# Decode block: part of the last gate's weights loaded early on ScalarE's queue, and ScalarE's eight groups written as a loop

## The chip, the cores and the metric

The kernel runs on one core of a Trainium2 chip. The metric is the time of one execution on the device, in microseconds (us). The engines are named as the profile names them: PE multiplies matrices (PEld is its loading of weights), DVE is the vector engine, ACT the scalar engine, POOL and SP the two others. SP issues nearly all transfers here. Every transfer is cut into rows, and the rows are spread over 16 DMA engines, which work side by side.

## The reference

One decode step (one new token for each of 4 sequences) through attention with a cache and a gated feed-forward layer, both modulated by a condition `c`:

```python
x = A_x                                                   # 4 x 1 x 512
mod = (_silu(c) @ w_mod).reshape(c.shape[0], 6, 1, -1)    # 512 x 3072 weights
sa, ca, ga, sb, cb, gb = (mod[:, i] for i in range(6))
h = _layernorm(x) * (1 + ca) + sa
x = x + ga * attention(h)      # 32 heads of 128 in 8 groups, last 2048 of the cached keys
h = _layernorm(x) * (1 + cb) + sb
x = x + gb * ((_silu(h @ w1) * (h @ w3)) @ w2)            # 1792 hidden columns
```

All numbers are float32. What makes it long is the reading: keys and values of 8 groups (8 x 8 MB), the projections, and the weights of the two layers, each read once.

## The kernel before, in words

**Stages.** `t0_in` (the condition `c` and the weights of the first two gates) comes first, on SP's queue; the query weights `t1_in` and the input `x` come on ACT's queue. Then SP loads keys and values of one group after the other into two buffers, `KV[0]` and `KV[1]`, 8 MB each and so of 128 rows of 64 KB, and the projections of two groups at a time into `WP`. After the last group come, in this order and all on SP's queue: `wm_in` (three gates), `f1_in`, `f2_in` in two parts (the feed-forward layer's first weights), `gb_in` (the last gate, `gb`: 128 rows of 2048 numbers), and `w2_in` in six parts (semaphores `dw0` to `dw5`). The answer leaves with one small transfer.

**What holds a load back.** SP waits before a load until its buffer is free. Before the change it counts `q_done` (PE has projected the queries, so the query weights in `WP` may go) and `o_done` (PE has finished with the values, so a `KV` buffer may go).

**One group.** PE multiplies queries and keys (`scores`, into the accumulator `bS`), DVE finds the maxima and passes their negatives on as `NB`, ACT takes the exponent (`p_sb`), PE transposes (`bP`), DVE copies to `pT`, PE multiplies with the values (`values`, into `bO`), ACT divides by the sums (`o_sb`, with `LB` of DVE), PE transposes (`bX`, counted by `x_done`), and PE projects out (`proj_out`). ACT also scales the queries (`q_sb`) that PE has projected into `bQ`; PE transposes them (`bT`, counted by `qt_done`). PE runs the groups in a loop over four pairs (the blocks `query` and `pair`, with `take`, which waits for a semaphore and takes its count away again). DVE and ACT have all eight groups written out, and the last branch leads every engine to the block `post`.

**The end.** In `post` PE multiplies the condition with the last gate's weights into `bM` (four products of 512 columns, one for each 128 of the condition's 512 numbers, each to its own four rows), ACT copies that to `gb_sb`, and PE sums the four parts into `bT`, which ACT copies to `gbJ`. The products with `w2_in` follow part by part as they land; the last part releases the last products into `bX`, then DVE's two last operations (`yt`, `y`) and the transfer of the answer.

Of the kernel before, what the change touches and what calls it, by code (L numbers as in the profile page):

```python
# [14 lines left out]
EPS = 1e-5  # L15
CHUNKS = [(j, c) for c in range(4) for j in range(4) if c < 2 or j < 3]
HEAD = 8
W2_CUTS = [0, 4, 8, 10, 12, 13, 14]
PAIRS = G // 2

# [20 lines left out]
        return (self.sem, self.n)  # L41


def block_kernel(nc, x_in, t0_in, t1_in, kv_in, w_in, wm_in, f1_in, f2_in, gb_in, w2_in, out):
    T, v, s, gp, S = nc.tensor, nc.vector, nc.scalar, nc.gpsimd, nc.sync

    def sems(names):
        return [nc.alloc_semaphore(n) for n in names.split()]

    def sb(name, cols, rows=P):  # L50
        return nc.alloc_sbuf_tensor(name, (rows, cols), F32).ap()
# [5 lines left out]
    A = Queue(nc, s, "act")  # L57
    V = Queue(nc, v, "dve")
    L = Queue(nc, gp, "pool")
    dx, dt0, dt1, dkv, dk, dva, dvb, dwo, dm, df1, df2a, df2b, dgb = sems("dx dt0 dt1 dkv dk dva dvb dwo dm df1 df2a df2b dgb")  # L60
    dw = sems(" ".join(f"dw{i}" for i in range(len(W2_CUTS) - 1)))
    z_ok, q_ok, p_ok, k_ok, va_ok, vb_ok, pt_ok, o_ok, ot_ok = sems("z_ok q_ok p_ok k_ok va_ok vb_ok pt_ok o_ok ot_ok")
    s_done, q_done, qt_done, pp_done, o_done, x_done, a_done, pe, last = sems("s_done q_done qt_done pp_done o_done x_done a_done pe last")
    (dout,) = sems("dout")

    KV = [sb("KV0", 16384), sb("KV1", 16384)]
    WP = sb("WP", 8192)
    T0 = KV[1][:, : 16 + 4096]
    x_sb = sb("x_sb", 512, B)
    ident, same, eps = sb("ident", P), sb("same", B), sb("eps", 1)  # L70
    sc, e1, e2 = sb("sc", 16), sb("e1", 16), sb("e2", 16)
    hT, h2T = sb("hT", 16), sb("h2T", 16)
    Z = sb("Z", B * 28)
    q_sb, p_sb, o_sb, a_sb, y_sb, g_sb, u_sb, gb_sb = [sb(n, 512) for n in "q_sb p_sb o_sb a_sb y_sb g_sb u_sb gb_sb".split()]
# [10 lines left out]
    bS, bQ, bT, bP, bO, bX, bA, bM = [bank(n) for n in "bS bQ bT bP bO bX bA bM".split()]  # L85


    def load(dst, src, sem):
        S.dma_start(dst, src).then_inc(sem, 16)  # L89

    load(T0, t0_in, dt0)
    s.dma_start(WP[:, 4096:], t1_in).then_inc(dt1, 16)
    s.dma_start(x_sb, x_in).then_inc(dx, 16)
    load(KV[0], kv_in[0], dkv)
    S.wait_ge(pe, 1)
    load(KV[1], kv_in[1], dk)
    for p in range(PAIRS):
        if p == PAIRS - 1:
            break
        S.wait_ge(q_done, 2 * p + 2)  # L100
        if p:
            S.wait_ge(a_done, 2 * p)
        if p < PAIRS - 2:
            load(WP, w_in[p], dwo)
        else:
            load(WP, w_in[p], dwo)
        S.wait_ge(o_done, 2 * p + 1)
        load(KV[0], kv_in[2 * p + 2], dkv)
        S.wait_ge(o_done, 2 * p + 2)
        if p < PAIRS - 2:  # L110
            load(KV[1], kv_in[2 * p + 3], dk)
    S.wait_ge(a_done, G - 2)
# [1 line left out]
    load(KV[1][:, :8192], kv_in[G - 1][:, :8192], dk)  # L114
    load(KV[1][:, 8192:14336], kv_in[G - 1][:, 8192:14336], dva)
    load(KV[1][:, 14336:], kv_in[G - 1][:, 14336:], dvb)
    S.wait_ge(o_done, G - 1)
    load(KV[0][:, :6144], wm_in, dm)
    load(KV[0][:, 6144:14336], f1_in, df1)
    S.wait_ge(o_done, G)  # L120
    load(KV[1][:, :3072], f2_in[:, :3072], df2a)
    load(KV[1][:, 3072:6144], f2_in[:, 3072:], df2b)
    load(KV[1][:, 6144:8192], gb_in, dgb)
    for a, b, sem in zip(W2_CUTS[:-1], W2_CUTS[1:], dw):
        load(KV[1][:, 8192 + a * 512 : 8192 + b * 512], w2_in[:, a * 512 : b * 512], sem)

# [52 lines left out]
    v_same = V.op(v.tensor_reduce(same, ident.rearrange("p (j i) -> p i j", i=32)[:, :B, :], axis=AX.X, op=ALU.add))  # L179

    A.wait((dt0, 16))
    t = A.op(s.activation(e1, T0[:, :16], AF.Exp, scale=-1.0))
    V.wait(t)
    t = V.op(v.tensor_scalar(e2, e1, 1.0, None, op0=ALU.add))
    V.wait(t)
    t = V.op(v.reciprocal(e2, e2))
    V.wait(t, (dt0, 16))
    t_sc = V.op(v.tensor_mul(sc, T0[:, :16], e2))  # L188

    A.wait((pe, 1))  # L190
    t_sa = A.op(s.copy(sa_sb, bM[32 : 32 + B, :]))
# [3 lines left out]
    t_h = V.op(v.scalar_tensor_tensor(h, xs, st1[:, 7:8], sa_sb, op0=ALU.mult, op1=ALU.add))  # L195
    V.wait((pe, 2))
    t_hT = V.op(v.tensor_copy(hT, bT[:, :16]))  # L197

    def q_evac(g):
        A.wait((q_done, g + 1), v_z)  # L200
        A.op(s.mul(q_sb, bQ, DH**-0.5), q_ok)  # L201

    def q_place(g):
        V.wait((qt_done, g + 1), l_z)
# [15 lines left out]
    def weights(g):  # L220
        V.wait((s_done, g + 1), l_z)
        t = V.op(v.reduce_max(MX[:, 0:1], bS, axis=AX.X))  # L222
        V.wait(t)
        t = V.op(v.transpose(MT, MX))
        V.wait(t)
        t = over_t(NM, MT, ALU.max, negate=True)
        V.wait(t)
        t_nm = V.op(v.transpose(NB, NM))  # L228
        A.wait(t_nm)
        A.op(s.activation(p_sb, bS, AF.Exp, bias=NB[:, 0:1], accum_out=SM[:, 0:1]), p_ok)  # L230
        if g % 2 == 0:
            q_evac(g + 1)
        V.wait((pp_done, g + 1))
        V.op(
            v.tensor_copy(  # L235
                pT.rearrange("p (t b c r) -> p c b t r", t=NT, b=B, c=4),
                bP.rearrange("p (c b i) -> p c b i", c=4, b=B)[:, :, :, :16].rearrange("p c b (t r) -> p c b t r", t=NT),
            ),
            pt_ok,
        )  # L240
        if g % 2 == 0:
            q_place(g + 1)
        t = V.op(v.transpose(ST, SM))
        V.wait(t)
        t = over_t(LS, ST, ALU.add)
        V.wait(t)
        t = V.op(v.reciprocal(LR[:, :16], LS[:, :16]))
        V.wait(t)
        t_lb = V.op(v.transpose(LB, LR))
        A.wait((o_done, g + 1), t_lb)  # L250
        A.op(s.mul(o_sb, bO, LB[:, 0:1]), o_ok)  # L251
        V.wait((x_done, g + 1))
        diag = bass.AP(bX.tensor, bX.offset, [list(bX.ap[0]), [1, R], [32, B], [132, 4]])
        V.op(v.tensor_reduce(oT.rearrange("p (r b) -> p r b", r=R), diag, axis=AX.X, op=ALU.add), ot_ok)  # L254
        if g % 2 and g < G - 1:
            q_evac(g + 1)
            q_place(g + 1)

    q_evac(0)
    q_place(0)  # L260
    for g in range(G):
        weights(g)
# [2 lines left out]
    def mm(o, lhsT, rhs, start=True, stop=True):  # L265
        return T.matmul(o, lhsT, rhs, start=start, stop=stop, skip_group_check=True)  # L266
# [38 lines left out]
        ins.then_inc(a_done, 1)  # L305

    root = nc.cur_bb
    reg = T.alloc_register("pairs")
    T.reg_mov(reg, 0)
    T.wait_ge(L.sem, l_z[1])  # L310
    mm(bA, zero[:, :P], zero)
    T.wait_ge(V.sem, t_sc[1])
    for k in range(4):
        for i in range(2):
            ins = mm(bM[32 * i : 32 * i + B, :], sc[:, k * B : (k + 1) * B], T0[:, 16 + (2 * k + i) * 512 : 16 + (2 * k + i + 1) * 512], k == 0, k == 3)
    ins.then_inc(pe, 1)
    T.wait_ge(V.sem, t_h[1])
    for k in range(4):
# [2 lines left out]
    T.wait_ge(V.sem, t_hT[1])  # L321
    T.wait_ge(dt1, 16)
    nc.br("query", engines=[ET.PE])
    nc.br("post", engines=[ET.Activation, ET.DVE, ET.Pool, ET.SP])

    with nc.body("pair", parent=root, valid_engines=[ET.PE]):
        T.reg_add(reg, reg, 1)
# [32 lines left out]
    with nc.body("leave", parent=root, valid_engines=[ET.PE]):  # L360
        T.wait_ge(V.sem, V.n + 1)
        mm(bM[:B, :], same, a_sb).then_inc(pe, 1)
        nc.br("post", engines=[ET.PE])


    nc.switch_bb("post", parent=root)
# [74 lines left out]


    T.wait_ge(dgb, 16)
    for k in range(4):
        ins = mm(bM[32 * k : 32 * k + B, :], sc[:, k * B : (k + 1) * B], KV[1][:, 6144 + 512 * k : 6144 + 512 * (k + 1)])
    ins.then_inc(pe, 1)
    A.wait((pe, 10))
    t_gb = A.op(s.copy(gb_sb, bM))
# [38 lines left out]
def _layout(i):  # L487
    import numpy as np

    def a(t):  # L490
        return np.ascontiguousarray(t)

    k = i["A_k_cache"][:, :, SK - W :, :].reshape(B, G, NT, 512, DH)
    v = i["A_v_cache"][:, :, SK - W :, :].reshape(B, G, NT, 4, P, DH)
    k = k.transpose(1, 4, 2, 0, 3).reshape(G, P, 8192)
    v = v.transpose(1, 4, 2, 0, 3, 5).reshape(G, P, 8192)
    wm = i["w_mod"].reshape(4, P, 6, 512).transpose(1, 0, 2, 3)
    c = i["c"].reshape(B, 4, P).transpose(2, 1, 0).reshape(P, 16)
    wq = i["A_wq"].reshape(4, P, G, 512).transpose(2, 1, 0, 3).reshape(G, P, 2048)
    wo = i["A_wo"].reshape(G, R, P, D).transpose(0, 2, 1, 3).reshape(G, P, 2048)  # L500
    pairs = [[wo[2 * p], wo[2 * p + 1]] + ([wq[2 * p + 2], wq[2 * p + 3]] if p < 3 else [wo[6], wo[7]]) for p in range(4)]
    w1 = i["B_w1"].reshape(4, P, FF).transpose(1, 0, 2)
    w3 = i["B_w3"].reshape(4, P, FF).transpose(1, 0, 2)
    w2 = i["B_w2"].reshape(14, P, D)
    return {
        "x_in": a(i["A_x"].reshape(B, D)),
        "t0_in": np.concatenate([c, wm[:, :, 1::-1].reshape(P, 4096)], 1),
        "t1_in": np.concatenate([wq[0], wq[1]], 1),
        "kv_in": np.concatenate([k, v], 2),
        "w_in": np.stack([np.concatenate(p, 1) for p in pairs]),  # L510
        "wm_in": a(wm[:, :, 2:5]).reshape(P, 6144),
        "f1_in": np.concatenate([w1, w3[:, :, 1536:]], 2).reshape(P, 8192),
        "f2_in": a(w3[:, :, :1536]).reshape(P, 6144),
        "gb_in": a(wm[:, :, 5]).reshape(P, 2048),
        "w2_in": a(np.stack([w2[4 * j + c_] for j, c_ in CHUNKS], 1)).reshape(P, 14 * D),
    }

# [14 lines left out]
```

## Time and profile before

| | us |
|---|---|
| median of 3 runs | 243.2 (243.02 to 243.39) |
| the profiled execution, its own time | 243.09 |
| its span in the profile | 241.7 |

The span is the stretch that the profile shows; 1.4 us of the profiled execution's own time lie around it. In the rows below a start is in microseconds from the span's begin. "DMA share" in a table of windows is the mean busy share of the 16 DMA engines (it counts a packet in the window in which it starts, so single windows can exceed 1), and GB/s is what they moved. SPq and ACTq stand for the issue of transfers by SP and ACT. "q1", "q10", "q8" and "q14" are DMA queues: q1 is SP's, q10 ACT's, and q8 and q14 carry blocks of the program's own instructions.

### The profile page before, as it was taken

What the parts mean: (1) busy time and instruction counts of PE and PEld (TensorE: products, weight loads), DVE (VectorE), ACT (ScalarE), POOL (GpSimd) and SP (SyncE); (2) the same over time, 40 slices, a digit from 0 to 9 for tenths busy, and PEclk for the clock granted to TensorE, in tenths of its full rate; (3) what the DMA queues carried; (4) which work ended last, traced back from release to release, by engine and by line L of the source; (5) the groups of instructions that cost most, each with busy time, mean ns of one, the idle gap of its engine ahead of it and who ended that gap; (6) DMA issues with size and microseconds to landing.
All of it is one profiled execution on the core that took longest, in us unless ns stands there. A gap on an engine that the chain in (4) does not pass through costs nothing. (4 is left out here: it accounts for less than half of the span.)

```text
span 241.7 us, 2238 instructions
## 1 busy us (share of the span) xinstructions
PE 137.8 (57%) x940; PEld 38.0 (16%) x940; DVE 38.6 (16%) x126; ACT 25.1 (10%) x54; POOL 1.7 (1%) x14
## 2 busy tenths in 40 slices
PE   3004677726771478267713782877137869656964
PEld 0000122201220013112200130121001312111211
DVE  3003203202200022022000220130002222133112
ACT  2002002100010011010100110011002100133110
POOL 2000000000000000000000000000000000000000
PEclk9999959968798579887985898679758997995999
DMA  7998989899989898999898989998989999999993
GB/s 266 440 511 358 510 361 499 369 423 439 504 369 499 369 499 370 423 428 504 369 499 369 499 369 423 434 510 369 499 347 445 442 396 445 449 431 394 413 415 116
DMA packets 4045, 101.34 MB, mean 419 GB/s; under 512 B 452, under 2 KB 580, under 8 KB 1096
## 3 DMA queue, kind: packets, MB, share of 16 engines
q1 hardware_dynamic: 3888, 99.17, 95.7%
q10 hardware_dynamic: 152, 2.11, 2.1%
q8 instruction: 3, 0.05, 0.1%
q14 instruction: 2, 0.02, 0.0%
HBM read 101.20 MB, written 0.07 MB: 419 GB/s over the span
## 5 line engine op out<-in xcount | busy, mean ns | idle before, releaser
L266 PE MATMUL bS<-KV,Z 128*16 128x512 f32 x256 | 42.7, 828 | 39.2 <-PEq L269 39.2
L266 PE MATMUL bO<-KV,pT 128*16 128x512 f32 x256 | 32.5, 652 | 0.5
L266 PEld LDWEIGHTS bS<-KV,Z 128*16 128x16 f32 x256 | 9.3, 123 | 67.1 <-issue 67.1
L222 DVE TENSOR_REDUCE MX<-bS 128x1 f32<-128x512 f32 x8 | 5.5, 692 | 80.4 <-PE bS L266 80.4
L266 PE MATMUL bM<-KV,sc 128*4 128x512 f32 x24 | 6.9, 801 | 16.6 <-DVE sc L188 16.6
L230 ACT ACTIVATE p_sb<-bS,NB 128x512 f32<-128x512 f32 x8 | 5.5, 687 | 101.2 <-DVE NB L228 101.2
L287 PE MATMUL bP<-ident,p_sb 128*128 128x128 f32 x32 | 5.6, 303 | 16.6 <-PEq L269 16.6
L266 PE MATMUL bA<-WP,oT 128*4 128x512 f32 x64 | 11.1, 773 | 4.3 <-PEq L269 4.3
L266 PEld LDWEIGHTS bO<-KV,pT 128*16 128x16 f32 x256 | 8.2, 107 | 23.9 <-issue 23.9
L251 ACT ACTIVATE o_sb<-bO,LB 128x512 f32<-128x512 f32 x8 | 5.5, 687 | 48.8 <-PE bO L266 48.8
L266 PE MATMUL bQ<-WP,hT 128*4 128x512 f32 x64 | 9.2, 647 | 0.6 <-DVE hT L197 0.6
L287 PE MATMUL bX<-ident,o_sb 128*128 128x128 f32 x32 | 5.0, 280 | 7.2 <-PEq L269 7.2
L254 DVE TENSOR_REDUCE oT<-bX 128x16 f32<-128x64 f32 x8 | 1.8, 224 | 43.6 <-PE bX L287 43.6
L287 PEld LDWEIGHTS bP<-ident,p_sb 128*128 128x128 f32 x32 | 3.6, 148 | 24.0 <-issue 24.0
L287 PE MATMUL bT<-ident,q_sb 128*128 128x128 f32 x32 | 5.5, 298 | 3.2 <-PEq L269 3.2
L201 ACT ACTIVATE q_sb<-bQ 128x512 f32<-128x512 f32 x8 | 4.7, 593 | 13.3 <-PE bQ L266 13.3
L287 PEld LDWEIGHTS bX<-ident,o_sb 128*128 128x128 f32 x32 | 3.4, 141 | 14.3 <-issue 14.3
L235 DVE COPY pT<-bP 128x256 f32<-128x256 f32 x8 | 3.4, 424 | 13.5 <-PE bP L287 13.5
L266 PE MATMUL bQ<-KV,h2T 128*4 128x512 f32 x32 | 5.3, 816 | 0.3 <-DVE h2T L398 0.3
L287 PEld LDWEIGHTS bT<-ident,q_sb 128*128 128x128 f32 x32 | 3.6, 150 | 8.0 <-issue 7.7
L266 PEld LDWEIGHTS bM<-KV,sc 128*4 128x4 f32 x24 | 1.0, 104 | 22.4 <-DVE sc L188 18.2
L266 PE MATMUL bX<-KV,sc 128*4 128x512 f32 x24 | 4.2, 592 | 0.0
(100 smaller groups left out, 65.2 us busy)
## 6 DMA issues: line engine op xcount, KB each, us to landing
WP<-w_in SPq DMA_DIRECT2D x3, 4096.0 KB, 22.0
KV<-kv_in SPq DMA_DIRECT2D x1, 4096.0 KB, 24.3
KV<-f_in SPq DMA_DIRECT2D x1, 4096.0 KB, 28.0
KV<-kv_in SPq DMA_DIRECT2D x1, 3072.0 KB, 31.1
KV<-wm_in SPq DMA_DIRECT2D x1, 3072.0 KB, 18.4
KV<-f_in SPq DMA_DIRECT2D x2, 1536.0 KB, 19.2
KV<-t_in SPq DMA_DIRECT2D x1, 2056.0 KB, 12.2
WP<-t_in ACTq DMA_DIRECT2D x1, 2048.0 KB, 12.4
```

What stands on the lines that cost most here:

```text
L201: A.op(s.mul(q_sb, bQ, DH**-0.5), q_ok)
L222: t = V.op(v.reduce_max(MX[:, 0:1], bS, axis=AX.X))
L230: A.op(s.activation(p_sb, bS, AF.Exp, bias=NB[:, 0:1], accum_out=SM[:, 0:1]), p_ok)
L235: v.tensor_copy(pT.rearrange("p (t b c r) -> p c b t r", t=NT, b=B, c=4), bP.rearrange("p (c b i) -> p c b i", c=4, b=B)[:, :, :, :16].rea ...
L251: A.op(s.mul(o_sb, bO, LB[:, 0:1]), o_ok)
L254: V.op(v.tensor_reduce(oT.rearrange("p (r b) -> p r b", r=R), diag, axis=AX.X, op=ALU.add), ot_ok)
L266: return T.matmul(o, lhsT, rhs, start=start, stop=stop, skip_group_check=True)
L287: ins = T.transpose(dst[:, c * P : (c + 1) * P], src[:, c * P : (c + 1) * P], ident)
```

## The change

Three things are changed.

1. Of the last gate's weights (512 rows, one for each number of the condition, by 512 columns) the last 192 columns of rows 128 to 511 are taken out of `gb_in`. They come as `gc_in`, four blocks of 96 rows by 192 columns, on ACT's queue behind `x`, into a buffer `GC` of 96 partitions. `gb_in` keeps 320 columns of all four blocks and 192 more of the first, so its rows shrink from 2048 numbers to 1472. In memory `gc_in` has 12 parts of 9 rows, of which 8 are loaded. The condition comes a second time, cut into 96s (`t0_in` has 16 columns more, and `sc`, `e1`, `e2` are 32 wide).
2. PE makes the last gate with nine products in place of four, and waits for `GC` too (`dgc`).
3. ACT's eight groups become a loop over four pairs, the block `act_pair`. Since it takes the counts of `q_done` and `o_done` away again, SP counts `qt_done` and `x_done` instead, which PE raises later.

```diff
+GA = 320
+GB = 512 - GA
...
     s.dma_start(x_sb, x_in).then_inc(dx, 16)
+    s.dma_start(GC, gc_in[:, :8]).then_inc(dgc, 16)
     load(KV[0], kv_in[0], dkv)
...
-        S.wait_ge(q_done, 2 * p + 2)
+        S.wait_ge(qt_done, 2 * p + 2)
...
-        S.wait_ge(o_done, 2 * p + 1)
+        S.wait_ge(x_done, 2 * p + 1)
         load(KV[0], kv_in[2 * p + 2], dkv)
-        S.wait_ge(o_done, 2 * p + 2)
+        S.wait_ge(x_done, 2 * p + 2)
...
-    S.wait_ge(o_done, G)
+    S.wait_ge(x_done, G)
     load(KV[1][:, :3072], f2_in[:, :3072], df2a)
     load(KV[1][:, 3072:6144], f2_in[:, 3072:], df2b)
-    load(KV[1][:, 6144:8192], gb_in, dgb)
+    load(KV[1][:, 6144 : 6144 + 4 * GA + GB], gb_in, dgb)
...
+    with nc.body("act_pair", parent=root, valid_engines=[ET.Activation]):
+        s.reg_add(areg, areg, 1)
+        for odd in range(2):
+            if not odd:
+                atake(q_done)
+                A.op(s.mul(q_sb, bQ, DH**-0.5), q_ok)
+            atake(nm_ok)
+            A.op(s.activation(p_sb, bS, AF.Exp, bias=NB[:, 0:1], accum_out=SM[:, 0:1]), p_ok)
+            if not odd:
+                atake(q_done)
+                A.op(s.mul(q_sb, bQ, DH**-0.5), q_ok)
+            atake(lb_ok, o_done)
+            A.op(s.mul(o_sb, bO, LB[:, 0:1]), o_ok)
+        s.br_lt(areg, PAIRS, on_true="act_pair", on_false="post")
...
     T.wait_ge(dgb, 16)
+    T.wait_ge(dgc, 16)
     for k in range(4):
-        ins = mm(bM[32 * k : 32 * k + B, :], sc[:, k * B : (k + 1) * B], KV[1][:, 6144 + 512 * k : 6144 + 512 * (k + 1)])
+        mm(bM[32 * k : 32 * k + B, :GA], sc[:, k * B : (k + 1) * B], KV[1][:, 6144 + GA * k : 6144 + GA * (k + 1)])
+    mm(bM[:B, GA:], sc[:, :B], KV[1][:, 6144 + 4 * GA : 6144 + 4 * GA + GB], True, False)
+    for k in range(4):
+        ins = mm(bM[32 * k : 32 * k + B, GA:], sc[:96, 16 + k * B : 16 + (k + 1) * B], GC[:, GB * k : GB * (k + 1)], k > 0, True)
...
+    gc = np.zeros((12, 9, 4 * GB), wg.dtype)
+    gc[:, :8] = i["w_mod"][P:, 5 * 512 + GA : 6 * 512].reshape(4, 96, GB).transpose(1, 0, 2).reshape(12, 8, 4 * GB)
```

How the instructions stand is shown at two places. The first is ACT, from its last copy before the groups on. Before the change each of the eight groups has its rows; here stand the first three groups and the begin of the fourth:

```order
L191 COPY sa_sb<-bM 4x512
L201 ACTIVATE q_sb<-bQ 128x512
L230 ACTIVATE p_sb,SM<-bS,NB 128x512
L201 ACTIVATE q_sb<-bQ 128x512
L251 ACTIVATE o_sb<-bO,LB 128x512
L230 ACTIVATE p_sb,SM<-bS,NB 128x512
L251 ACTIVATE o_sb<-bO,LB 128x512
L201 ACTIVATE q_sb<-bQ 128x512
L230 ACTIVATE p_sb,SM<-bS,NB 128x512
L201 ACTIVATE q_sb<-bQ 128x512
```

After the change the same place reads as follows; the branch at the end leads back to the row of `L365`:

```order
L195 COPY sa_sb<-bM 4x512
L318 UNCONDITIONAL_BRANCH
L365 REGISTER_ALU
L369 ACTIVATE q_sb<-bQ 128x512
L371 ACTIVATE p_sb,SM<-bS,NB 128x512
L374 ACTIVATE q_sb<-bQ 128x512
L376 ACTIVATE o_sb<-bO,LB 128x512
L371 ACTIVATE p_sb,SM<-bS,NB 128x512
L376 ACTIVATE o_sb<-bO,LB 128x512
L377 COMPARE_AND_BRANCH
L391 COPY ga_sb<-bX 4x512
```

The order of ACT's work is the same; its program is 29 rows long in place of 45, with one more transfer at its head.

The second place is PE in `post`, around the last gate (`bM`, four rows for each product). Before:

```order
L437 MATMUL bS<-ident,u_sb 128x96 x4
L266 MATMUL bM<-KV,sc 4x512 x4
L266 MATMUL bO<-KV,hidT 4x512 x4
L266 MATMUL bT<-gb_sb,same 4x128 x4
L266 MATMUL bO<-KV,hidT 4x512 x4
L266 MATMUL bX<-KV,hidT 4x128 x8
```

And after:

```order
L451 MATMUL bS<-ident,u_sb 128x96 x4
L259 MATMUL bM<-KV,sc 4x320 x4
L259 MATMUL bM<-KV,sc 4x192
L259 MATMUL bM<-GC,sc 4x192 x4
L259 MATMUL bO<-KV,hidT 4x512 x4
L259 MATMUL bT<-gb_sb,same 4x128 x4
L259 MATMUL bO<-KV,hidT 4x512 x4
L259 MATMUL bX<-KV,hidT 4x128 x8
```

The nine products of the last gate stand where the four stood, and all that follows is the same, five products further down.

More of the change, by code (lines that the diff above doesn't have):

```diff
@@ L41, in op, with block_kernel @@
         return (self.sem, self.n)
-def block_kernel(nc, x_in, t0_in, t1_in, kv_in, w_in, wm_in, f1_in, f2_in, gb_in, w2_in, out):
+def block_kernel(nc, x_in, t0_in, t1_in, kv_in, w_in, wm_in, f1_in, f2_in, gb_in, gc_in, w2_in, out):
     T, v, s, gp, S = nc.tensor, nc.vector, nc.scalar, nc.gpsimd, nc.sync
@@ L63, in block_kernel @@
     s_done, q_done, qt_done, pp_done, o_done, x_done, a_done, pe, last = sems("s_done q_done qt_done pp_done o_done x_done a_done pe last")
-    (dout,) = sems("dout")
+    (nm_ok, lb_ok, dgc, dout) = sems("nm_ok lb_ok dgc dout")
     KV = [sb("KV0", 16384), sb("KV1", 16384)]
     WP = sb("WP", 8192)
-    T0 = KV[1][:, : 16 + 4096]
+    T0 = KV[1][:, : 32 + 4096]
     x_sb = sb("x_sb", 512, B)
+    GC = sb("GC", 4 * GB, 96)
     ident, same, eps = sb("ident", P), sb("same", B), sb("eps", 1)
-    sc, e1, e2 = sb("sc", 16), sb("e1", 16), sb("e2", 16)
+    sc, e1, e2 = sb("sc", 32), sb("e1", 32), sb("e2", 32)
     hT, h2T = sb("hT", 16), sb("h2T", 16)
@@ L116, in block_kernel @@
     load(KV[1][:, 14336:], kv_in[G - 1][:, 14336:], dvb)
-    S.wait_ge(o_done, G - 1)
+    S.wait_ge(x_done, G - 1)
     load(KV[0][:, :6144], wm_in, dm)
     load(KV[0][:, 6144:14336], f1_in, df1)
-    S.wait_ge(o_done, G)
+    S.wait_ge(x_done, G)
     load(KV[1][:, :3072], f2_in[:, :3072], df2a)
     load(KV[1][:, 3072:6144], f2_in[:, 3072:], df2b)
-    load(KV[1][:, 6144:8192], gb_in, dgb)
+    load(KV[1][:, 6144 : 6144 + 4 * GA + GB], gb_in, dgb)
     for a, b, sem in zip(W2_CUTS[:-1], W2_CUTS[1:], dw):
@@ L181, in block_kernel @@
     A.wait((dt0, 16))
-    t = A.op(s.activation(e1, T0[:, :16], AF.Exp, scale=-1.0))
+    t = A.op(s.activation(e1, T0[:, :32], AF.Exp, scale=-1.0))
     V.wait(t)
@@ L187, in block_kernel @@
     V.wait(t, (dt0, 16))
-    t_sc = V.op(v.tensor_mul(sc, T0[:, :16], e2))
+    t_sc = V.op(v.tensor_mul(sc, T0[:, :32], e2))
     A.wait((pe, 1))
@@ L197, in block_kernel @@
     t_hT = V.op(v.tensor_copy(hT, bT[:, :16]))
-    def q_evac(g):
-        A.wait((q_done, g + 1), v_z)
-        A.op(s.mul(q_sb, bQ, DH**-0.5), q_ok)
     def q_place(g):
@@ L227, in weights @@
         V.wait(t)
[L228 to L232, printed above, removed]
+        V.op(v.transpose(NB, NM), nm_ok)
         V.wait((pp_done, g + 1))
@@ L248, in weights @@
         V.wait(t)
-        t_lb = V.op(v.transpose(LB, LR))
-        A.wait((o_done, g + 1), t_lb)
-        A.op(s.mul(o_sb, bO, LB[:, 0:1]), o_ok)
+        V.op(v.transpose(LB, LR), lb_ok)
         V.wait((x_done, g + 1))
@@ L255, in weights @@
         if g % 2 and g < G - 1:
-            q_evac(g + 1)
             q_place(g + 1)
-    q_evac(0)
+    A.wait(v_z, l_z)
     q_place(0)
@@ L307, in block_kernel @@
     root = nc.cur_bb
-    reg = T.alloc_register("pairs")
+    reg, areg = T.alloc_register("pairs"), s.alloc_register("act_pairs")
     T.reg_mov(reg, 0)
+    s.reg_mov(areg, 0)
     T.wait_ge(L.sem, l_z[1])
@@ L314, in block_kernel @@
         for i in range(2):
-            ins = mm(bM[32 * i : 32 * i + B, :], sc[:, k * B : (k + 1) * B], T0[:, 16 + (2 * k + i) * 512 : 16 + (2 * k + i + 1) * 512], k == 0, k == 3)
+            ins = mm(bM[32 * i : 32 * i + B, :], sc[:, k * B : (k + 1) * B], T0[:, 32 + (2 * k + i) * 512 : 32 + (2 * k + i + 1) * 512], k == 0, k == 3)
     ins.then_inc(pe, 1)
@@ L323, in block_kernel @@
     nc.br("query", engines=[ET.PE])
-    nc.br("post", engines=[ET.Activation, ET.DVE, ET.Pool, ET.SP])
+    nc.br("act_pair", engines=[ET.Activation])
+    nc.br("post", engines=[ET.DVE, ET.Pool, ET.SP])
     with nc.body("pair", parent=root, valid_engines=[ET.PE]):
@@ L363, in block_kernel, with atake @@
         nc.br("post", engines=[ET.PE])
+    def atake(*sems_):
+        for s_ in sems_:
+            s.wait_ge(s_, 1).then_inc(s_, -1)
+    with nc.body("act_pair", parent=root, valid_engines=[ET.Activation]):
[12 more added lines that the diff above has]
+        s.br_lt(areg, PAIRS, on_true="act_pair", on_false="post")
     nc.switch_bb("post", parent=root)
@@ L498, in _layout @@
     c = i["c"].reshape(B, 4, P).transpose(2, 1, 0).reshape(P, 16)
+    c96 = np.zeros((P, 16), c.dtype)
+    c96[:96] = i["c"].reshape(B, 512)[:, P:].reshape(B, 4, 96).transpose(2, 1, 0).reshape(96, 16)
+    wg = wm[:, :, 5]
+    gc = np.zeros((12, 9, 4 * GB), wg.dtype)
+    gc[:, :8] = i["w_mod"][P:, 5 * 512 + GA : 6 * 512].reshape(4, 96, GB).transpose(1, 0, 2).reshape(12, 8, 4 * GB)
     wq = i["A_wq"].reshape(4, P, G, 512).transpose(2, 1, 0, 3).reshape(G, P, 2048)
@@ L506, in _layout @@
         "x_in": a(i["A_x"].reshape(B, D)),
-        "t0_in": np.concatenate([c, wm[:, :, 1::-1].reshape(P, 4096)], 1),
+        "t0_in": np.concatenate([c, c96, wm[:, :, 1::-1].reshape(P, 4096)], 1),
         "t1_in": np.concatenate([wq[0], wq[1]], 1),
@@ L513, in _layout @@
         "f2_in": a(w3[:, :, :1536]).reshape(P, 6144),
-        "gb_in": a(wm[:, :, 5]).reshape(P, 2048),
+        "gb_in": np.concatenate([a(wg[:, :, :GA]).reshape(P, 4 * GA), wg[:, 0, GA:]], 1),
+        "gc_in": gc,
         "w2_in": a(np.stack([w2[4 * j + c_] for j, c_ in CHUNKS], 1)).reshape(P, 14 * D),
```

## The prediction

> **What bounds the kernel now.** I read the page's DMA parts first, then the chain that ended last, then the end in small windows. From the page:
>
> ```profile
> span 241.7 us, 2238 instructions
> ...
> DMA  7998989899989898999898989998989999999993
> ...
> q1 hardware_dynamic: 3888, 99.17, 95.7%
> q10 hardware_dynamic: 152, 2.11, 2.1%
> q8 instruction: 3, 0.05, 0.1%
> q14 instruction: 2, 0.02, 0.0%
> ```
>
> The 16 DMA engines are busy from end to end (the two data queues hold 97.8% of their time), while no compute engine is. The chain that ended last says the same of the last microseconds (columns: start, length, what):
>
> ```profile
> 210.14 28.79 DMA KV<-w_in
> 238.97 0.45 PE bX L266 x8
> 239.44 0.30 DVE yt L478
> 239.77 0.29 DVE y L480
> ```
>
> The last part of `w2_in` is seen to have landed at 238.93; what follows it (2.7 us to the span's end) is fixed. So only the landing of the last byte counts. How the engines come to their end is seen in windows (the last two columns are DMA share and GB/s):
>
> ```profile
> 100.00:200.00 100.00, 59.01 (x403) 16.75 (x404) 13.74 (x48) 8.82 (x18) 0.00 (x0) 0.81 1.00 431
> 235.00:236.00 1.00, 0.84 (x8) 0.11 (x8) 0.00 (x0) 0.00 (x0) 0.00 (x0) 1.00 0.99 389
> 237.00:237.25 0.25, 0.25 (x12) 0.11 (x8) 0.00 (x0) 0.00 (x0) 0.00 (x0) 1.00 0.35 131
> 237.25:237.50 0.25, 0.17 (x8) 0.00 (x0) 0.00 (x0) 0.00 (x0) 0.00 (x0) 1.00 0.25 98
> 237.50:237.75 0.25, 0.04 (x4) 0.04 (x8) 0.00 (x0) 0.00 (x0) 0.00 (x0) 1.00 0.19 74
> 237.75:238.00 0.25, 0.25 (x12) 0.24 (x16) 0.00 (x0) 0.00 (x0) 0.00 (x0) 1.00 0.15 57
> 238.00:238.25 0.25, 0.25 (x13) 0.04 (x4) 0.00 (x0) 0.00 (x0) 0.00 (x0) 1.00 0.13 49
> 238.25:238.50 0.25, 0.22 (x12) 0.11 (x8) 0.00 (x0) 0.00 (x0) 0.00 (x0) 1.00 0.07 25
> 238.50:238.75 0.25, 0.25 (x8) 0.00 (x0) 0.00 (x0) 0.00 (x0) 0.00 (x0) 1.00 0.00 0
> ```
>
> With all 16 at work on small rows they move 389 GB/s, 24.3 each. Divided by that, the windows from 237.25 on have 4.0, 3.0, 2.3, 2.0 and 1.0 engines at work, then none. So twelve engines are done by about 237.2, and four are late: they end near 237.5, 237.85, 238.25 and 238.5 (PE sees the last end 0.4 us later, at 238.93). The kernel waits for the last of them, 1.3 us behind the bulk.
>
> What made them late? The instruction packets fit. One row each of five windows, 33 to 36, 91.5 to 93, 206 to 207.5, 213 to 215.5 and 236.9 to 237.1 us (last column: share of 16 engines' time in the window):
>
> ```profile
> q8 instruction: 1, 0.02, 2.1%
> ...
> q14 instruction: 1, 0.01, 1.4%
> ...
> q14 instruction: 1, 0.01, 1.3%
> ...
> q8 instruction: 1, 0.02, 2.7%
> ...
> q8 instruction: 1, 0.02, 34.2%
> ```
>
> Share x 16 x window: the q8 packets hold one engine for 1.0, 1.1 and 1.1 us, the q14 packets for 0.3 us each. Four of the five come before the tail, and four engines are late there. That each belongs to one late engine is my inference; no view names the engines.
>
> **The change part by part.** *What leaves the tail.* A row of `gb_in` loses 576 numbers, 2304 bytes. 128 rows on 16 engines are 8 rows each, 18.4 KB; at 431/16 = 26.9 GB/s that is 0.68 us less for every engine.
>
> *What comes early.* `GC` is 96 rows of 3072 bytes, the same sum of bytes. Over 16 engines it would cost each 0.68 us again, and nothing would be gained. But its source has 12 parts of 8 rows. That the count of parts sets the number of engines is seen at q10: its 152 packets are the 128 rows of `t1_in` with 16 closing packets, and the 4 rows of `x` with 4. So I take 12 engines, each with 24.6 KB, 0.91 us. With 64 bytes more in each of `t0_in`'s rows (8 x 64 bytes, 0.02 us), twelve engines end 0.25 us later than before and four end 0.66 us earlier. Which engines get it no row shows.
>
> *Which four are spared* decides. If all four late ones: the end moves from 238.5 to 237.84, or -0.66. If the last two only, the third late engine ends at 237.85 + 0.25 = 238.1: -0.40. If the last one isn't among them: +0.25. The packets that made engines late came on two queues, for different engines' programs, so I expect the two q8 engines (the heavier packets, and so the last two) to be alike and a q14 engine to be elsewhere: -0.40.
>
> *ACT's loop.* The q14 packet at 206 to 207.5 falls where ACT goes on after a long wait; PE is at its matmuls, and the only other engine that goes on there is SP, with a program of 27 transfers:
>
> ```profile
> 206.46 0.69 ACT L251 ACTIVATE o_sb<-bO,LB 128x512 f32<-128x512 f32 x1 [6.89 <-PE bO L266]
> ...
> 207.29 0.63 PE L287 MATMUL bX<-ident,o_sb 128*128 128x128 f32 x4 [0.91 <-PEq L269]
> ```
>
> With 29 rows in place of 45, ACT should not need that block. That is 0.3 us or somewhat more off one engine; I price it at 0, since an engine that a q14 packet made late isn't the last. That a loop of its own may fetch at each turn is a rival below.
>
> *Later issues.* `x_done` comes after ACT's 0.69 and PE's four transposes: from 206.45 to 207.92, 1.5 us after `o_done`. `qt_done` comes 2.7 us after `q_done` (89.20 to 91.90):
>
> ```profile
> 89.20 0.33 SPq L89 DMA_DIRECT2D WP<-w_in  x1
> 90.53 0.59 ACT L201 ACTIVATE q_sb<-bQ 128x512 f32<-128x512 f32 x1
> 91.27 0.63 PE L287 MATMUL bT<-ident,q_sb 128*128 128x128 f32 x4
> ```
>
> The cover is the queue ahead (last column: us from issue to landing):
>
> ```profile
> WP<-w_in SPq DMA_DIRECT2D x3, 4096.0 KB, 22.0
> KV<-kv_in SPq DMA_DIRECT2D x7, 32.2
> KV<-f_in SPq DMA_DIRECT2D x2, 1536.0 KB, 19.2
> ```
>
> At 431 GB/s 4096 KB take 9.7 us, 8192 KB 19.5, the two parts of `f_in` 7.3: each load stands 12 us or more in the queue before its first byte moves. 2.7 us fit in; if they didn't, each load would start late by the excess and the end with it. Cost 0.
>
> *The start.* `GC`'s rows share the engines with `KV[0]`'s first load, which lands up to 0.91 us later, at about 33.3 (`t0_in`, issued in the first microsecond, lands 12.2 us later, and 8192 KB at 431 GB/s take 19.5 more: 32.4). The scores wait for DVE's `Z` until 33.85, so this is covered too, and past it by the queue:
>
> ```profile
> KV<-t_in SPq DMA_DIRECT2D x1, 2056.0 KB, 12.2
> ...
> 33.51 0.23 DVE L206 TENSOR_REDUCE Z<-bT 128x16 f32<-128x64 f32 x1 [4.22 <-PE bT L287]
> 33.85 0.18 PEld L266 LDWEIGHTS bS<-KV,Z 128*16 128x16 f32 x8 [0.78 <-issue]
> ```
>
> *PE's nine products.* Four take 1.04 us as 8 matmuls and 8 loads; nine are 18 and 18, of 2240 columns for 2048: at most 0.36 us more at the pace of the 16 pairs in 0.58 us (236.44 to 237.02). PE then waits for `w2_in` for 1.1 us twice, so it costs 0:
>
> ```profile
> 231.47 1.04 PE L266 MATMUL bM<-KV,sc 128*4 128x512 f32 x8
> ...
> 235.16 1.04 PE L266 MATMUL bO<-KV,hidT 128*4 128x512 f32 x8 [1.14 <-DMA KV<-w_in]
> ...
> 236.44 0.33 PEld L266 LDWEIGHTS bX<-KV,hidT 128*4 128x4 f32 x16 [1.17 <-DMA KV<-w_in]
> ...
> 237.02 0.11 PEld L266 LDWEIGHTS bX<-y_sb,same 128*4 128x4 f32 x8 [0.25 <-DVE y_sb L471]
> ```
>
> *Sum.* -0.40 on the profiled execution's 243.09 gives 242.7; the median of the runs is 243.2, so 242.8 against it. This kernel's measurement can tell about 0.2%, 0.5 us, from no change, so I forecast a small gain that may not be told from none.
>
> **The rivals.** *All late engines are spared* (0.13): -0.66, 242.5. For it: four late, four spared. Against it: two queues.
>
> *The last engine isn't spared* (0.26): it gets the 0.25 and the end moves to 238.75, 243.45. Nothing in a view excludes it; four of sixteen are spared.
>
> *The last instruction packet becomes the end* (0.14), slower. At 236.9 to 237.1 a q8 packet holds an engine for 1.1 us until 238.1, and harms nobody: that engine's data were over. It comes as PE reaches a place in its program near the row of 237.02. Twenty instructions more ahead of that place make PE reach it some 0.36 us earlier in the stretch, near 236.6. If it then falls on one of the twelve, which have data until 237.2 + 0.25, that engine ends at 237.45 + 1.1 = 238.55, and up to 0.4 later if its next rows start slowly: 243.2 to 243.6. It decides from 1.05 us of hold on.
>
> *Nothing is rebalanced* (0.07): the load spreads over 16 engines, 243.2. [...]
>
> *ACT's loop fetches at each turn* (0.02): four turns, each a q14 packet of 0.3 us on some engine; if all fall on the engine that is last in the forecast, 238.1 + 1.2 = 239.3 and 243.9, if on others, nothing. It decides from two packets on that engine. PE's loop of four pairs speaks against it: the page has three q8 packets in all, and two of them, at 213 and 237, come after the loop. [...]
>
> **How the numbers follow.** Forecast 0.38, the rivals 0.13, 0.26, 0.14, 0.07 and 0.02. Faster by over 0.2% (under 242.7): most of the 0.13 and two fifths of the 0.38, by scatter: 0.27. Slower (over 243.7): a sixth of the 0.26, a third of the 0.14, and the 0.02: 0.11. Same: 0.62. The range reaches from the full rebalance with 0.1 of scatter, 242.4, to the end packet's upper end, 243.6.
>
> **What would show it.** q10 with 152 + 96 + 12 = 260 packets and one q14 packet instead of two; the last landing 0.4 us earlier; two or three engines in the window before it, not one. One late engine ending later than 238.5, or a q8 packet among the last data, would make me wrong, and so would a DMA row that falls below 9 before the tail.

## The result, and the profile after

The changed kernel takes 244.74 us (median of 6 executions, 243.54 to 245.09), the kernel before on the same chip 243.09 (242.85 to 243.39): a ratio of 1.0063, with an interval of 1.0047 to 1.0078. It is slower, where a gain of 0.4 us was forecast. The profiled execution is the one of 243.54, at the lower end of the six: its profile shows 0.45 us of a loss that is 1.65 at the median, and what follows explains that execution.

The page of the changed kernel, its DMA parts (for a queue: packets, MB, share of 16 engines):

```profile
span 242.2 us, 2293 instructions
...
DMA  7998998989998989899999998999989999999993
...
q1 hardware_dynamic: 3888, 98.88, 95.5%
q10 hardware_dynamic: 260, 2.40, 2.4%
q8 instruction: 3, 0.05, 0.1%
q14 instruction: 1, 0.01, 0.0%
```

The counts are the forecast ones: 260 packets on q10, one q14 packet in place of two. The DMA row is as full as before. The end of the chain that ended last (start, length, what):

```profile
213.73 25.75 DMA KV<-w_in
239.47 0.04 issue
239.52 0.45 PE bX L259 x8
239.96 0.02 issue
239.99 0.30 DVE yt L496
240.29 0.02 issue
240.31 0.29 DVE y L498
```

It is the same chain, but the last landing is seen at 239.47, not 238.93: 0.54 later. The windows of the end (the last two columns are DMA share and GB/s) say how the 16 engines finish:

```profile
237.00:237.25 0.25, 0.24 (x12) 0.24 (x16) 0.25 (x1) 0.00 (x0) 0.00 (x0) 1.00 1.11 426
237.75:238.00 0.25, 0.24 (x8) 0.00 (x0) 0.00 (x0) 0.00 (x0) 0.00 (x0) 1.00 0.92 352
238.00:238.25 0.25, 0.00 (x0) 0.00 (x0) 0.00 (x0) 0.00 (x0) 0.00 (x0) 1.00 0.45 164
238.25:238.50 0.25, 0.20 (x8) 0.20 (x12) 0.00 (x0) 0.00 (x0) 0.00 (x0) 1.00 0.22 82
238.50:238.75 0.25, 0.25 (x16) 0.13 (x7) 0.00 (x0) 0.00 (x0) 0.00 (x0) 1.00 0.15 57
238.75:239.00 0.25, 0.25 (x12) 0.09 (x8) 0.00 (x0) 0.00 (x0) 0.00 (x0) 1.00 0.06 25
239.00:239.25 0.25, 0.25 (x8) 0.02 (x7) 0.00 (x0) 0.00 (x0) 0.00 (x0) 1.00 0.00 0
```

Two things are to be seen. The last engine now ends at about 239.0, some 0.8 us behind the bulk (238.2), where it was 1.3 behind: the load was rebalanced. But the bulk itself ends 1 us later than before (237.2), though each engine had 0.66 us less or 0.25 us more to move. Somewhere the engines lost time without being idle.

Where is seen at the start. The queue q1 from 14 to 34 us, while `GC` comes in on q10: ahead of the change, then after it:

```profile
q1 hardware_dynamic: 146, 8.52, 98.3%
...
KV<-kv_in SPq DMA_DIRECT2D x1, 25.6
```

```profile
q1 hardware_dynamic: 144, 8.39, 101.4%
q10 hardware_dynamic: 108, 0.29, 3.9%
...
KV<-kv_in SPq DMA_DIRECT2D x1, 27.0
```

Divide the MB by the time that the packets held an engine (share x 16 x 20 us). Before, a key row moved at 27.1 GB/s; after, at 25.9. The share is full in both: the rows were not queued longer, each took longer. The packet records of the trace give the same without a window: a row of 64 KB takes 2.418 us before; after, most take 2.50 to 2.64 (2.74 at most) while `GC`'s rows lie between (they start from 14.5 to 35.9 us), then 2.42 again. Added up over the first 16 rows of an engine, and taken on average over the 16 engines, the excess over 2.418 is 0.04 us before and 1.01 after. From 60 to 200 us both run at 27.0 (60.34 MB at 99.9%, 60.64 at 100.3%).

The sum then closes: the forecast -0.40 and the excess of 0.97 give +0.57; the last landing moved by 0.54. (The -0.40 is the forecast's and not measured by itself.)

### The profile page after: what moved, and what is told of

Read it like the earlier page. It is cut to its first block, busy times and chain, and to the rows that moved or that the text cites. A ratio compares the mean times of both kernels' runs of the same rounds, so it can differ in the third digit from the quotient of the medians.

```text
span 242.2 us, 2293 instructions
## 1 busy us (share of the span) xinstructions
PE 135.1 (56%) x950; PEld 37.8 (16%) x950; DVE 38.8 (16%) x126; ACT 25.1 (10%) x54; POOL 1.7 (1%) x14
## 5 line engine op out<-in xcount | busy, mean ns | idle before, releaser
L259 PE MATMUL bS<-KV,Z 128*16 128x512 f32 x256 | 43.6, 842 | 42.9 <-PEq L262 42.9
L259 PE MATMUL bO<-KV,pT 128*16 128x512 f32 x256 | 31.7, 638 | 0.5
L259 PE MATMUL bM<-KV,sc 128*4 128x512 f32 (+2 forms) x26 | 6.4, 672 | 16.8 <-DVE sc L192 16.8
L259 PE MATMUL bA<-WP,oT 128*4 128x512 f32 x64 | 10.2, 715 | 3.7 <-PEq L262 3.7
L259 PE MATMUL bQ<-WP,hT 128*4 128x512 f32 x64 | 8.4, 592 | 0.6 <-DVE hT L201 0.6
L280 PE MATMUL bT<-ident,q_sb 128*128 128x128 f32 x32 | 5.0, 279 | 3.6 <-PEq L262 3.6
L206 DVE TENSOR_REDUCE Z<-bT 128x16 f32<-128x64 f32 x8 | 1.8, 225 | 14.1 <-PE bT L280 13.8
```

The lines of the kernel that those rows point to most:

```text
L206: v.tensor_reduce(Z.rearrange("p (b i) -> p b i", b=B)[:, :, 12 : 12 + R], bT.rearrange("p (r k i) -> p i r k", r=R, k=4)[:, :B], axis=AX. ...
L280: ins = T.transpose(dst[:, c * P : (c + 1) * P], src[:, c * P : (c + 1) * P], ident)
```

## The experiments

**Which part.** The changed kernel once more; the loop and the later counts alone, with `gb_in`, `t0_in` and the four products as before the change; and `GC` alone, with the old counts and ACT's groups written out. Against the changed kernel, the loop alone:

```diff
-    s.dma_start(GC, gc_in[:, :8]).then_inc(dgc, 16)
...
-    load(KV[1][:, 6144 : 6144 + 4 * GA + GB], gb_in, dgb)
+    load(KV[1][:, 6144:8192], gb_in, dgb)
```

`GC` alone:

```diff
-        S.wait_ge(qt_done, 2 * p + 2)
+        S.wait_ge(q_done, 2 * p + 2)
...
-        S.wait_ge(x_done, 2 * p + 1)
+        S.wait_ge(o_done, 2 * p + 1)
...
-    nc.br("act_pair", engines=[ET.Activation])
-    nc.br("post", engines=[ET.DVE, ET.Pool, ET.SP])
+    nc.br("post", engines=[ET.Activation, ET.DVE, ET.Pool, ET.SP])
```

> The changed kernel as it is, for a second profile and more times, since its profiled execution took 243.5 and five others 244.5 to 245.1. Contention theory (ACT's rows of GC between the rows of the first keys slow all 16 engines by about 1 us in all, and nothing else is lost): the loss is the same in every execution, so times near 243.6, and the spread stays open. Compute theory (keys and values land 1.4 us later, the last group ends 2 us later, and PE's chain after it has eaten up its two waits of 1.1 us, so that PE and its clock set the end in most executions): times of 244.5 to 245, and in a profile of such an execution PE waits nowhere for the last parts of w2 and starts the last products over 0.5 us after the landing. End-packet theory (the last q8 packet falls on an engine that still has data): such a profile shows a q8 packet among the last landings and the last landing 1 us later than 239.0.

> The kernel before with ACT's loop and the later counts (qt_done, x_done), and without GC. Contention theory: equal to before, 243.1, or 0.3 us faster where the q14 packet mattered. Compute theory in the form that the loop costs (more waits of ACT in each group, 2 us over the groups): 243.5 or more, with the last group ending later than in the kernel before although its values land at the same time. One q14 packet instead of two in either case.

> The kernel before with GC early, and ACT's groups written out, SP counting q_done and o_done as before. Contention theory: as slow as the changed kernel's profiled execution or a little slower, 243.5 to 243.8, since all the loss is GC's. Compute theory with the loop as its cause: clearly faster than the changed kernel, 243.2 to 243.6, where the changed kernel takes 244.7. Compute theory with the late landing as its cause: like the changed kernel, 244.5.

Measured: again 244.1 (ratio 1.0046, 1.0029 to 1.0062), with an excess of 1.27 in its profile (one loss, the same in every execution, had been expected); the loop alone 243.07 (0.9998, 0.9989 to 1.0008), with one q14 packet; `GC` alone 244.29 (1.0055, 1.0038 to 1.0072), with two. So the loss comes with `GC`. The loop and the counts that SP gets later cost nothing, and the q14 packet that the loop saves gains nothing, as the prediction priced them. In neither profile of the changed kernel does PE set the end: in both, the last products still wait 0.2 us for the last part of `w2_in`.

**Twelve engines or sixteen, a second queue or one.** Four forms of the changed kernel. `GC` as 96 plain rows, so that 16 engines carry 6 each (264 packets on q10):

```diff
-    s.dma_start(GC, gc_in[:, :8]).then_inc(dgc, 16)
+    s.dma_start(GC, gc_in).then_inc(dgc, 16)
```

`GC` on SP's queue ahead of the first keys, so that it has a turn of its own:

```diff
-    s.dma_start(GC, gc_in[:, :8]).then_inc(dgc, 16)
+    load(GC, gc_in[:, :8], dgc)
     load(KV[0], kv_in[0], dkv)
```

`GC` on SP's queue in the tail:

```diff
-    s.dma_start(GC, gc_in[:, :8]).then_inc(dgc, 16)
...
     load(KV[1][:, 6144 : 6144 + 4 * GA + GB], gb_in, dgb)
+    load(GC, gc_in[:, :8], dgc)
```

And `GC` twice on ACT's queue, the copy in `GC2` never read:

```diff
+    s.dma_start(GC2, gc_in[:, :8]).then_inc(dgc2, 16)
     s.dma_start(GC, gc_in[:, :8]).then_inc(dgc, 16)
```

> GC comes from 96 plain rows, so that it should spread over 16 engines, 6 rows each; all else is as in the changed kernel. Contention theory: the KV rows beside it are as slow as in the changed kernel (390 GB/s in 12.4 to 32 us where the kernel before has 435), the time is the changed kernel's within 0.3 us. Imbalance theory (the time is lost on the twelve engines): the four engines that end first are gone from the tail, and the time falls to 243.2 or lower. Compute theory: the last keys and values land 0.2 us earlier than in the changed kernel, so 0.2 us faster at most.

> GC's load of 12 parts on SP's queue, ahead of the first keys, so that its rows stand in line with the keys' and not between them. Both contention theories: 27 GB/s for the keys' rows in 14 to 34 us; nothing but the intended shift is left, so the last landing comes 0.4 us ahead of the kernel before's, as the prediction's sum has it, and the time is 242.6 to 242.9. Imbalance theory (twelve engines run 0.9 us behind four, and that alone costs): 244 as in the changed kernel. If the foreign partitions cost by themselves, not only between other rows, GC's own rows are slower than 0.12 us each.

> GC's load of 12 parts on SP's queue right behind the last gate's other weights: the bytes stay in the tail, but twelve engines carry them. Four engines are 0.66 us earlier and twelve 0.25 us later, as the prediction has it, with nothing between the keys. Contention theories: 27 GB/s in 14 to 34 us and 242.6 to 242.9; the last keys and values land as in the kernel before, so PE keeps its waits of 1.1 us ahead of the second part of w2. If the third rival of the prediction (the last instruction packet) matters, up to 243.5.

> The changed kernel with GC loaded twice, first into a buffer that nobody reads, both behind x on ACT's queue; the first copy's bytes are added work, 0.9 us on twelve engines. Contention theories: the keys' rows are slow for twice as long (25.9 GB/s also in 36 to 50 us, where the changed kernel is back at 27), so another 1 us beside the 0.9: 245.8 to 246.3. If the loss has another cause and only bytes count: 245.0 to 245.3.

Measured: 16 engines 244.03 (1.0046, 1.0028 to 1.0064), own turn 244.06 (1.0039, 1.0027 to 1.005), in the tail 244.7 (1.0072, 1.0055 to 1.0089), twice 246.98 (1.0153, 1.0135 to 1.0171). The engines' number isn't it. Nor is the place: wherever these 295 KB come into 96 partitions, and in whichever queue, about 1 us or more is lost; for its own turn and for the tail 242.6 to 242.9 had been expected, and both missed. Twice the load loses more than twice, and more than the 246.3 that was the upper end of what had been expected. With its own turn the excess sits in `GC`'s own rows (0.171 us on average, 0.305 at most, where they took 0.130 in the changed kernel) and in the first keys behind it (2.93 on average). In the tail it sits in `gb_in` and its neighbours (from 228 to 230 us a row of 8192 bytes takes 0.54 us, where it took 0.31 in the kernel before); the windows of that kernel, then of the kernel before:

```profile
226.00:228.00 2.00, 1.43 (x13) 0.45 (x10) 0.00 (x0) 0.00 (x0) 0.00 (x0) 1.00 1.04 341
228.00:230.00 2.00, 1.87 (x13) 0.28 (x12) 1.20 (x5) 0.22 (x1) 0.00 (x0) 1.00 1.05 242
230.00:232.00 2.00, 1.01 (x12) 0.59 (x13) 0.82 (x2) 0.00 (x0) 0.00 (x0) 1.00 0.97 368
```

```profile
226.00:228.00 2.00, 1.74 (x15) 0.47 (x10) 0.00 (x0) 0.40 (x1) 0.00 (x0) 1.00 0.99 412
228.00:230.00 2.00, 2.00 (x16) 0.43 (x14) 1.13 (x4) 0.22 (x1) 0.00 (x0) 1.00 1.04 434
230.00:232.00 2.00, 1.20 (x15) 0.47 (x12) 0.89 (x2) 0.00 (x0) 0.00 (x0) 1.00 0.99 414
```

Full engines, and fewer GB/s. (A packet counts in the window in which it starts, so a single window says little, three in a row more.)

**The same bytes in another form.** 144 columns of all four blocks, as 128 rows of 2304 bytes into 128 partitions, on ACT's queue behind `x` as before. That its rows are dealt to the engines as the keys' rows are was the author's assumption, from the like form of the two loads; no record names the partitions of an engine. Against the changed kernel:

```diff
-GA = 320
+GA = 368
-    GC = sb("GC", 4 * GB, 96)
+    GC = sb("GC", 4 * GB)
-    s.dma_start(GC, gc_in[:, :8]).then_inc(dgc, 16)
+    s.dma_start(GC, gc_in).then_inc(dgc, 16)
```

> The same bytes early on ACT's queue behind x, but as 128 rows of 2304 bytes (the last 144 columns of all four blocks) into 128 partitions, so that each engine's rows of GC go to the same partitions as its rows of the keys. The keys' rows moved 27.1 GB/s for each busy engine in 14 to 34 us in the kernel before, 25.9 in the changed kernel, 25.5 in its second profile, 26.0 with GC on 16 engines. Foreign-partition theory (GC's rows of 96 partitions go to partitions that are other engines' in the loads of 128): 27 GB/s again, and the time falls to the kernel before's, 243.0 to 243.2. Second-queue theory (small rows of a second queue between the large ones slow all): 25.9 GB/s as before and about 244.

Measured: 243.09 (1.0000, 0.999 to 1.0009). Its q1 from 14 to 34 us:

```profile
q1 hardware_dynamic: 144, 8.39, 96.9%
q10 hardware_dynamic: 144, 0.29, 3.8%
```

27.1 GB/s with 0.29 MB of another queue in between: sharing the engines with this second queue cost the keys' rows nothing. What differs from the run with 16 engines is the number of partitions, 128 for 96, and for each engine the rows' size and number (8 of 2304 bytes for 6 of 3072).

**The same partitions, the same number of engines, cut otherwise.** Next `GC` was made 64 partitions with six blocks of 192 columns, in two kernels. In the first, two loads of 32 partitions each have eight parts of four rows; in the second one load has eight parts of eight rows. Taken that each part has an engine of its own, as the 12 closing packets on q10 for the 12 parts of the changed kernel let one think, eight engines carry eight rows of 4608 bytes each in both. The theory in the expectations rests on one more assumption of the author's: that in the first an engine writes partitions that it also writes for the keys, and in the second partitions that other engines write for them. No record names engines or partitions. The first against the second:

```diff
     GC = sb("GC", 6 * GB, 64)
...
-    s.dma_start(GC, gc_in[:, :8]).then_inc(dgc, 16)
+    s.dma_start(GC[:32], gc_in[:8, :4]).then_inc(dgc, 16)
+    s.dma_start(GC[32:], gc_in[8:, :4]).then_inc(dgc, 16)
```

> The same 295 KB as two loads of 32 partitions (rows of 4608 bytes, 8 parts of 4 rows each, so 8 engines with 4 rows of each load), on ACT's queue behind x, with the loop. [...] Theory (a row slows the others when it goes to partitions that belong to another engine): the keys' rows keep their 2.42 us beside GC, 27.0 GB/s per engine in 14 to 34 us. Eight engines get 8 x 4608 bytes, 1.37 us, and lose 0.68 in gb's rows: +0.69; the other eight -0.68. If the third late engine is among the spared, 242.4 to 242.6, if not, 243.0 to 243.3. Rival (any load over fewer than 128 partitions, or over fewer than 16 engines, slows the others): 25.9 GB/s or less, and 243.8 to 244.6.

> [...] The sums of bytes of every engine are those of the run with two loads of 32 partitions. Theory (a row slows the others when it goes to partitions that belong to another engine): the keys' rows take 2.5 to 2.65 us while GC comes, 25.9 GB/s per engine or less in 14 to 34 us, and 0.7 to 1.4 us more than the run with two loads: 243.4 to 244.5. Rival (any load over fewer than 128 partitions slows the others): the same time and rate as the run with two loads, within 0.2 us.

Measured: 243.32 (1.0015, 1.0005 to 1.0024) and 244.79 (1.0074, 1.0061 to 1.0087). The first's q1 and q10 from 14 to 34 us, and when its first keys had landed, then the second's:

```profile
q1 hardware_dynamic: 147, 8.59, 99.1%
q10 hardware_dynamic: 72, 0.27, 3.3%
...
KV<-kv_in SPq DMA_DIRECT2D x1, 25.5
```

```profile
q1 hardware_dynamic: 133, 8.00, 98.7%
q10 hardware_dynamic: 64, 0.27, 3.8%
...
KV<-kv_in SPq DMA_DIRECT2D x1, 28.3
```

27.1 GB/s against 25.3, for the same bytes, partitions, number of engines and queue. So it is not the 64 partitions, nor the eight engines: it is how the load is cut. The excess of the keys' rows is 0.07 us and 1.80 us, and `GC`'s own rows take 0.178 and 0.211 us on average. (The profiled executions lie further apart, 242.91 and 245.20, than the medians.) With the cut go the number of loads, how the rows lie in memory at the source and, perhaps, which partitions an engine writes; no run varies one of these alone. Of the first two, two loads of 96 partitions lost more than one (an excess of 3.23 for 1.01), and 96 plain rows lost about as much as 12 parts of 8 did (0.87 for 1.01). That the partitions make the difference remains the author's estimate: the outcome of the pair and of the 128 partitions agrees with it, and no record shows it.

By the packet records, joined as told below, all 16 engines were slowed in the changed kernel, also the four without a row of `GC`: their first keys ended at 32.2 to 32.5 us, where in the kernel before all engines' did at 31.4 to 31.9. No run shows by what a row of `GC` slows an engine that carries none.

In six runs the time of the profiled execution can be added up from the excess in its own records:

| kernel | excess, us | other terms, us | sum | profiled execution, us |
|---|---|---|---|---|
| changed | 1.01 | -0.40 | 243.7 | 243.54 |
| changed, again | 1.27 | -0.40 | 243.9 | 244.03 |
| `GC` alone | 0.98 | -0.40 | 243.6 | 243.63 |
| 16 engines | 0.87 | 0 (nothing rebalanced) | 243.9 | 244.00 |
| twice | 3.23 | -0.40 + 0.91 (12 engines, once more) | 246.8 | 247.17 |
| 128 partitions | 0.03 | 0 | 243.1 | 243.08 |

The sum is 243.09 + excess - 0.04 + other terms. It holds to 0.15 us but for the doubled load. For the pair it doesn't close: the first kernel's 242.91 and the difference of the two excesses, 1.73, give 244.64 for the second, which took 245.20; the other 0.56 us is not explained. (With its own turn and in the tail, the excess is not in the first 16 rows alone, so these two have no row here.)

**Without the loss: how much does rebalancing give?** In the first kernel of the pair the last landing is at 238.85, only 0.08 earlier than before. By the packet records its last engine ends at 238.40 and the next at 237.99 (the expectation below speaks of two at 238.40, but from 238.00 to 238.25 the DMA share is 0.06, one engine of 16). That the last one carries `GC` is the likeliest way to join the records, not shown. With 128 columns early the two sides should meet:

```diff
-GA = 320
+GA = 384
```

> As the run with two loads of 32 partitions, but 128 columns come early in place of 192 (GA = 384): rows of 3072 bytes in GC, 6656 in gb. Eight engines then get 0.46 us more than before and eight 0.46 less, where it was 0.69. In the run with 192 columns the records of the packets end at 238.40 on two engines of the eight that carry GC, and at 237.91 on the latest of the eight spared. Theory (each engine keeps to its own partitions, so only the sums of bytes count): 238.40 - 0.23 = 238.17 on the one side, 237.91 + 0.23 = 238.14 on the other, against 238.5 before: 0.3 us faster than before, 242.7 to 242.9; keys' rows at 27.0 GB/s in 14 to 34 us. Rival (what 192 columns gained in bytes and lost elsewhere is lost to instruction packets that fall on engines still at work, not to bytes): no better than the run with 192 columns, 243.2 to 243.4, with executions that differ by 0.8 us among themselves.

Measured: 242.95 (242.72 to 243.6) against 243.11, the ratio 0.9999 (0.999 to 1.0008). The profiled execution, 242.85, does what was expected:

```profile
238.00:238.25 0.25, 0.23 (x12) 0.11 (x8) 0.00 (x0) 0.00 (x0) 0.00 (x0) 1.00 0.11 41
238.25:238.50 0.25, 0.25 (x8) 0.00 (x0) 0.00 (x0) 0.00 (x0) 0.00 (x0) 1.00 0.00 0
...
238.69 0.04 issue
238.73 0.45 PE bX L260 x8
```

Two engines are last together (packet records: 238.16 and 238.27, where 238.17 and 238.14 were expected), and the landing comes 0.24 earlier than before. Of the 11 executions, seven lie between 242.72 and 242.97, two near 243.1 and two near 243.6; the interval does not tell it from the kernel before. No version beat that kernel beyond its measurement.

**Still open.** Why the changed kernel's executions spread over 1.5 us where those of before spread over 0.5; two profiles of it show excesses of 1.01 and 1.27, so the loss itself varies, but they are of executions of 243.54 and 244.03; no profile shows one of 244.5 to 245.1, and what these lose beyond it stays open. And in the kernel with two loads of 32 partitions five of the 12 executions lie between 242.9 and 243.05, three near 243.4 and four near 243.8 or above. An instruction packet on an engine that still has data would fit, but only one execution of each kernel has a profile, and it was not tried.

## Why the prediction was wrong

*The bound* was read right: the DMA engines, and of them the last landing. In all kernels the last products wait for it.

*Which four are spared* agrees with what was measured, but the records don't settle it. They name no engine; they can be joined packet by packet, since a row begins where the one before it on its engine ended, but rows of several engines often end within a few nanoseconds of each other. So joined, the engine of the first q8 packet (at 34.9 us) is among the four without `GC`, and that of the q14 packet (at 93.9) among the twelve; for the second q8 packet (at 215.5) the joining is not certain. The times fit: the forecast's last row at 238.1 and the 0.97 us of excess make 239.07, and the records end at 239.01.

*What comes early* is the step that failed, with *The start*. `GC` was priced by its bytes at 431/16 = 26.9 GB/s: 0.91 us for twelve engines, nothing for anyone else. Its own rows come near that (0.130 us each, 1.04 for eight). What was left out, a term put at nothing without a row to show it, is what they do to the rows beside them: +0.97 us for an engine on average in the profiled execution, 0.83 to 1.23 in the other profiles with one load of 96 partitions on ACT's queue. The 26.9 came from rows of loads of 128 partitions. The trace of before has no load of another shape under load but the 4 rows of `x`, so this price had no row; it was taken as known, where a bound from above was due. The runs show this step for the profiled executions; the rest of the 1.65 us at the median is open, as said above. *The start* said that the landing of the first keys is covered by `Z` and the queue. That holds for PE; but time that an engine loses inside a row is not a wait, and no queue covered it: it was carried to the end (a last landing 0.54 later), since the engines hardly rest (q1 and q10 hold 97.9% of their time).

*ACT's loop*, *Later issues* and *PE's nine products* were priced at 0 and cost 0: 243.07 without `GC`, 243.09 with nine products replaced by eight and `GC` in 128 partitions. But the cover of PE's products was read too large. PE does not wait 1.1 us twice: the second wait, 1.17, is that of its weight loads while PE still multiplies, and PE's own row has 0.24:

```profile
236.44 0.62 PE L266 MATMUL bX<-KV,hidT 128*4 128x128 f32 x16 [0.24 <-DMA KV<-w_in]
```

In the changed kernel the first wait, 1.14, is gone too; only the short ones for the last parts are left:

```profile
235.73 1.04 PE L259 MATMUL bO<-KV,hidT 128*4 128x512 f32 x8
237.01 0.62 PE L259 MATMUL bX<-KV,hidT 128*4 128x128 f32 x16 [0.23 <-DMA KV<-w_in]
...
239.52 0.40 PE L259 MATMUL bX<-KV,hidT 128*4 128x128 f32 x8 [0.20 <-DMA KV<-w_in]
```

So the DMA still sets the end in this execution, but little is left before PE would; whether it does in the longer executions no profile shows.

*The rivals.* None had this mechanism. That the last engine isn't spared came nearest by its time, 243.45, but its last row at 238.75 and the 0.97 us of excess would make 239.7, where the records end at 239.0. The last q8 packet comes in the window of 237.2 to 237.4 (share of 16 engines in the last column: 1.1 us), a little later than before and not earlier, and no row follows it in the records, so it found an engine that had finished:

```profile
q8 instruction: 1, 0.02, 34.6%
```

The rival in which that packet becomes the end took up to 0.4 us more for rows that start slowly behind it; this was an estimate of the author's, and no run shows it. What *Nothing is rebalanced* describes, bytes moved from the tail to the start for no gain, is seen in the run with 128 partitions on ACT's queue: a ratio of 1.0000.

*What would show it.* Both packet counts came true. Against the forecast stood the last landing, 0.5 us later and not 0.4 earlier, and one engine alone in the window before it (a DMA share of 0.06 from 238.75 to 239.00), ending later than 238.5. The DMA row did not fall below 9 more than before, and yet time was lost in it: from 14 to 34 us q1's share is 98.3% with 27.1 GB/s before and 101.4% with 25.9 after, so the busy share told that the engines held packets, not how fast the bytes moved.

## What to carry to other kernels

In a kernel bound by its transfers, divide bytes by busy time of each queue, window by window, before and after: here a full DMA row hid rows that took longer (27.1 and 25.9 GB/s at a share of 98.3 and 101.4%). Before a load is put beside large loads of 128 partitions, try more than one cut of it, and price a cut that no run has shown above its own bytes: here 295 KB, 0.68 us for an engine if spread evenly, cost nothing more as 128 rows or as two loads of 32 partitions, and up to 1.8 us more in the rows beside them as one load of 64 partitions. What a rebalancing by such a load can gain is bounded by how far the last engine is behind the bulk (1.3 us here), and it must be weighed against what the load does to every engine.

## What the runs showed of the hardware

- 295 KB as one load of 96 partitions, or of 64 in eight parts of eight rows, on a second queue beside the keys, cost the 16 engines 0.8 to 1.8 us each on average; the same 295 KB as 128 rows, or as two loads of 32 partitions in parts of four rows, cost no more than 0.03 us beyond the bytes (excess of 0.03 and 0.07, 0.04 without any).
- In the changed kernel most of the slowed rows take 3 to 13% longer (2.50 to 2.74 us for 2.418), and only while `GC`'s rows lie between. With `GC` in a turn of its own or in the tail it is more: 2.93 us on average for the first keys behind it, and 0.54 us for 0.31 in the tail.
- With the load doubled the loss more than doubled: an excess of 1.01 and 1.27 us with one `GC`, 3.23 with two.
- With ACT's groups as a loop of four turns and no `GC`, the profile has one q14 packet in place of two, and three q8 packets as before; 243.07 us against 243.04 on the same chip. (The second profile of the changed kernel has two q14 packets, of 0.01 MB together.)
